# Start phase of a Fourier mixing and Gelu network kernel: second table half later, its negation on GpSimd, the Gelu table loaded late, finer last copies

## The chip, the cores and the metric

The kernel runs on one core of one Trainium2 chip. The metric is the time of one execution on the device in microseconds (us), the median of several runs. TensorE (PE) multiplies matrices and writes into PSUM; VectorE (DVE), ScalarE (ACT) and GpSimd (POOL) work on elements; SyncE (SP) and GpSimd issue the transfers (DMA). Each engine takes its own instructions in order, and engines wait for each other by semaphores.

## The reference

The inputs are `x` (8 images of 3008 x 256), two filter tables of 1505 x 256, and two weight matrices.

```python
X = np.fft.rfft(x, axis=1)                      # x: (8, 3008, 256)
F = (filt_r + 1j * filt_i)[None, :, :]          # (1505, 256)
y = np.fft.irfft(X * F, n=3008, axis=1)
h = y.reshape(24064, 256) @ w_in                # w_in: (256, 2048)
g = 0.5 * h * (1.0 + erf(h / np.sqrt(2)))       # exact Gelu
out = g @ w_out                                 # w_out: (2048, 256), out in float32
```

## The kernel before

The transform of length 3008 = 47 x 64 is done as four table products: along 47 (c1), along 64 (c2, followed by the multiplication with the filters), back along 64 (c3), back along 47 (c4), with transposes between (c1t, c3t). The first image does this on the chip alone, in a start phase; later images do it with transfers through memory, between the matmuls of the network, which runs over 47 tiles of 512 rows (`mm1` with Gelu, `mm2`). The cosine and sine tables are made on the chip as well. Names like `T` or `ps_c` in the profile are these tiles with their numbers left out: `T` is any of T1 to T4.

The buffers in PSUM during the start phase: tag "w" has 2 buffers of two banks each, tag "n" has 4 buffers of one bank. A tag hands out its buffers in turn, and a buffer is free when its last reader is done.

```python
m.psum(wide, w=(2, 2), n=(4, 1))
```

The second table T2 has 24 rows k in two halves of 12. Each half is a sine on ScalarE, a swap (a matmul with a signed permutation, and two copies out of PSUM), and a negation:

```python
def table_2_sin(self, h):
    self.nc.scalar.activation(out=self.T2[:, 12*h:12*h+12, 1, :], in_=self.gen[:, h], func=AF.Sin, scale=2.0*PI)

def table_2_swap(self, h):
    t2 = self.T2[:, 12 * h:12 * h + 12]
    ps = self.bank("ps_sw", "w")
    for i in range(2):
        self.nc.tensor.matmul(ps[:, i, 0:384], lhsT=self.swap, rhs=t2[:, :, 1, 32*i:32*i+32], start=True, stop=True)
    for i in range(2):
        self._evac(t2[:, :, 2, 32*i:32*i+32], ps[:, i, 0:384].rearrange(...), "act", 1.0 - 2.0 * i)

def table_2_minus(self, h):
    t2 = self.T2[:, 12 * h:12 * h + 12]
    self.nc.vector.tensor_scalar(out=t2[:, :, 0, :], in0=t2[:, :, 2, :], scalar1=-1.0, scalar2=None, op0=ALU.mult)

def table_3(self, q, eng):         # 8 transposes of T2 rows into one bank, one copy out
    ps = self.bank("ps_t3", "n", BF16)
    ...
def table_4(self):                 # the weighted tables: 2 small matmuls, 2 small copies on ScalarE
    ps = self.bank("ps_t4", "n")
    ...
def warm_up(self, n):              # matmuls whose result nobody reads
    ps = self.bank("ps_warm", "n")
    for i in range(n):
        self.nc.tensor.matmul(ps, lhsT=self.ones[:, 0:128], rhs=self.ones, start=True, stop=True)
```

`_evac(out, in_, eng, scale)` copies out of PSUM: on ScalarE for "act", on VectorE for False. `dup_filters` copies filter rows from partitions 0-63 to 64-127, two values of k in one copy. The parts of the start phase (all of PSUM tag "n" but c2):

```python
def c1(self, grp, half, eng):      # 4 matmuls from the input x_sb, 1 copy into at_sb
def c1t(self, q, eng):             # 8 transposes of at_sb, 1 copy of 128x1024 into b_sb; needs all of c1
def c2(self, p):                   # 4 matmuls of T2 with b_sb, tag "w"; then the multiplication:
    ...
    if p < 11:
        nc.vector.tensor_tensor(out=w, in0=ps, in1=f..., op=ALU.mult)     # 128x1024
        return
    ...                            # p = 11: two multiplications of 128x512
def c3(self, q):                   # 16 matmuls of T3 with the results of c2(2q) and c2(2q+1)
    ps = [self.bank("ps_c3", "n") for half in range(2)]
    for i, half in ((0, 0), (1, 0), (0, 1), (1, 1), (2, 0), (3, 0), (2, 1), (3, 1)):
        w = self.st[0, "p", 2 * q + i // 2]
        o = 256 * (i % 2) + 128 * half
        for t in range(2):
            self.nc.tensor.matmul(ps[half][:, 128*i:128*i+128], lhsT=w[:, t, o:o+128], rhs=self.T3[:, 4*q+i]..., ...)
    for half in range(2):
        ...                        # one copy of 128x512 into vt_sb for each half
        self._evac(v[:, :, 16*q:16*q+16], ps[half]..., False if q == 5 and half else "act")
```

The order of the start phase:

```python
for k, n in ((0, 4), (4, 8), (12, 12)):
    m.load_filters(k, n)           # transfers issued by GpSimd
m.load_w_in()
...                                # T1p and T1q: two small copies on GpSimd
m.dup_filters(nc.gpsimd, 0, K1)
for u in range(16):
    m.c1(u // 2, u % 2, act if u < 4 or u % 2 and u != 15 else False)
    if u == 3:
        m.warm_up(3)
        m.table_2_sin(0)
    if u == 7:
        m.table_2_swap(0)
        m.table_2_minus(0)
    if u == 11:
        m.table_2_sin(1)
        nc.scalar.activation(out=warm, in_=m.p, func=AF.Gelu)    # brings the Gelu table in
m.load_x(1)                        # the next image, and w_out: transfers issued by GpSimd
m.load_w_out(0)
m.load_w_out(8)
m.c1t(0, False)
m.c1t(1, act)
for q in range(7):
    if q < 6:
        m.c2(2 * q)
        if q == 0:
            m.table_2_swap(1)
        if q + 2 < 6:
            m.c1t(q + 2, act)
        m.c2(2 * q + 1)
    if q == 1:
        m.table_2_minus(1)
    if q < 3:
        m.table_3(q, act)
    if q >= 1:
        m.c3(q - 1)
    if q == 5:
        m.table_4()
...                                # c3t, c4: back along 47; then the network with the other images
```

Of the kernel before, what the change touches and what calls it, by code (L numbers as in the profile page):

```python
# [9 lines left out]
AF = mybir.ActivationFunctionType  # L10
ALU = mybir.AluOpType
# [7 lines left out]
K1 = 24  # L19
HB = 32  # L20
# [8 lines left out]
class _Mix:  # L29
# [159 lines left out]

    def table_2_swap(self, h):  # L190
        t2 = self.T2[:, 12 * h:12 * h + 12]
        ps = self.bank("ps_sw", "w")
        for i in range(2):
            self.nc.tensor.matmul(ps[:, i, 0:384], lhsT=self.swap, rhs=t2[:, :, 1, 32 * i:32 * i + 32],
                                  start=True, stop=True)
        for i in range(2):
            self._evac(t2[:, :, 2, 32 * i:32 * i + 32], ps[:, i, 0:384].rearrange("p (k j) -> p k j", k=12),
                       "act", 1.0 - 2.0 * i)

    def table_2_minus(self, h):  # L200
        t2 = self.T2[:, 12 * h:12 * h + 12]
        self.nc.vector.tensor_scalar(out=t2[:, :, 0, :], in0=t2[:, :, 2, :], scalar1=-1.0, scalar2=None, op0=ALU.mult)

    def weights_4(self, g):

# [30 lines left out]

    def warm_up(self, n):

        ps = self.bank("ps_warm", "n")
        for i in range(n):  # L240
            self.nc.tensor.matmul(ps, lhsT=self.ones[:, 0:128], rhs=self.ones, start=True, stop=True)


    def _evac(self, out, in_, both, scale=None):
# [136 lines left out]
        for c in (slice(0, 128), slice(128, 256)):  # L381
            nc.vector.tensor_tensor(out=w[:, :, :, c], in0=ps[:, :, :, c], in1=f[:, :, :, c], op=ALU.mult)

    def c3(self, q):

        if q == 0:
            self.vt = self.pg.tile([128, 2, 97, 32], BF16, tag="g", name="vt_sb")
        ps = [self.bank("ps_c3", "n") for half in range(2)]
        for i, half in ((0, 0), (1, 0), (0, 1), (1, 1), (2, 0), (3, 0), (2, 1), (3, 1)):
            w = self.st[0, "p", 2 * q + i // 2]  # L390
            o = 256 * (i % 2) + 128 * half
            for t in range(2):
                self.nc.tensor.matmul(ps[half][:, 128 * i:128 * i + 128], lhsT=w[:, t, o:o + 128],  # L393
                                      rhs=self.T3[:, 4 * q + i].rearrange("p a b -> p (a b)"),
                                      start=t == 0, stop=t == 1)
        for half in range(2):
            v = self.vt[:, half, 0:96, :].rearrange("c a b -> c (a b)").rearrange("c (n k) -> c n k", n=HB)
            self._evac(v[:, :, 16 * q:16 * q + 16], ps[half].rearrange("c (k n) -> c n k", n=HB),
                       False if q == 5 and half else "act")

    def c3t(self, u):

# [69 lines left out]
@with_exitstack  # L472
def kernel(
    ctx: ExitStack,
    tc: tile.TileContext,
    x: bass.AP,
    filt_r: bass.AP,
    filt_i: bass.AP,
    moe_w_in: bass.AP,
    moe_w_out: bass.AP,  # L480
    out: bass.AP,
):
    m = _Mix(ctx, tc, x, filt_r, filt_i, moe_w_in, moe_w_out, out)
    nc, B, S = tc.nc, m.B, m.S
    NT = B * S // TCH
    ctx.enter_context(tc.manual_schedule())

    g = m.small
    wide = ctx.enter_context(ExitStack())
    m.psum(wide, w=(2, 2), n=(4, 1))  # L490
    act = "act"
    m.p = m.iota(g, "p", [128, 1], [[0, 1]], cm=1)
    m.load_x(0, 0, 1, (0,))
    m.pi = m.iota(g, "pi", [128, 1], [[0, 1]], cm=1, dt=I32)
    m.load_x(0, 0, 1, (1,))
    m.ones = g.tile([128, 512], BF16, name="ones")
    nc.vector.memset(m.ones, 1.0)
    m.warm_up(10)
    m.table_1(g)
    m.weights_4(g)  # L500
    m.T1c = g.tile([2 * NA, 96], BF16, name="T1c")
    nc.vector.tensor_copy(out=m.T1c.rearrange("p (k h r) -> p k h r", h=2, r=2),
                          in_=m.T1.rearrange("p (h r k) -> p k h r", h=2, r=2))
    m.kk = m.iota(g, "kk", [128, K1 // 2], [[1, K1 // 2]])
    m.jj = g.tile([128, NB], FP32, name="jj")
    for sgn, lo in ((1, 0), (-1, 32)):
        nc.gpsimd.iota(m.jj[:, lo:lo + 32], pattern=[[sgn * NA, 32]], base=min(0, sgn * NA),
                       channel_multiplier=0, allow_small_or_imprecise_dtypes=True)
    cols = m.iota(g, "cols", [128, 128], [[1, 128]])
    m.load_x(0, 1, 4)  # L510
    m.gen = m.py.tile([128, 3, K1 // 2, NB], FP32, tag="y", name="gen")
    m.table_2(g)
    m.table_2_angle(0)
    m.unit_matrices(g, cols)
    m.table_2_angle(1)
    for k, n in ((0, 4), (4, 8), (12, 12)):
        m.load_filters(k, n)
    m.load_w_in()
    m.T1p = g.tile([2 * NA, 2, K1, 2], BF16, name="T1p")
    nc.gpsimd.tensor_copy(out=m.T1p, in_=m.T1.rearrange("p (h r k) -> p h k r", h=2, r=2))  # L520
    m.T1q = g.tile([2 * NA, K1, 2, 2], BF16, name="T1q")
    nc.gpsimd.tensor_copy(out=m.T1q, in_=m.T1.rearrange("p (h r k) -> p k r h", h=2, r=2))
    m.dup_filters(nc.gpsimd, 0, K1)


    warm = g.tile([128, 1], FP32, name="warm")
    for u in range(16):
        m.c1(u // 2, u % 2, act if u < 4 or u % 2 and u != 15 else False)
        if u == 3:
            m.warm_up(3)  # L530
            m.table_2_sin(0)
        if u == 7:
            m.table_2_swap(0)
            m.table_2_minus(0)
        if u == 11:
            m.table_2_sin(1)

            nc.scalar.activation(out=warm, in_=m.p, func=AF.Gelu)
    m.load_x(1)
    m.load_w_out(0)  # L540
    m.load_w_out(8)
    m.c1t(0, False)
    m.c1t(1, act)
    for q in range(7):
        if q < 6:
            m.c2(2 * q)
            if q == 0:
                m.table_2_swap(1)
            if q + 2 < 6:
                m.c1t(q + 2, act)  # L550
            m.c2(2 * q + 1)
        if q == 1:
            m.table_2_minus(1)
        if q < 3:
            m.table_3(q, act)
        if q >= 1:
            m.c3(q - 1)
        if q == 5:
            m.table_4()
    wide.close()  # L560
    wide = ctx.enter_context(ExitStack())
    m.psum(wide, v=(5, 1), t=(3, 1))
    for u in range(10):
        if u < 8:
            m.c3t(u)
        if u >= 2:
            m.c4(u - 2, (act, False if u > 7 else act))
    wide.close()
    m.psum(ctx, h=(3, 1), o=(2, 1), f=(3, 1))


    at = {}

    def put(slot, f, *a):
        at.setdefault(slot, []).append((f, a))

    def first(b):
        return (b * S // TCH) * 16

    for b in range(1, B):  # L580
        hi = first(b)
        if b == 1:
            s1, n1, r1, s2, n2, r2, s4, n4 = 0, 1, 16, 26, 2.8, 61, 68, 0.72
        else:
            s1, n1, r1, s2, n2, r2, s4, n4 = hi - 94, 1, hi - 78, hi - 69, 3.7, hi - 23, hi - 17, 1
        for u in range(16):
            put(s1 + int(u * n1), m.s1, b, u)
            put(s4 + int(u * n4), m.s4, b, u // 2, u % 2)
        for c in range(4):
            put(r1, m.r1, b, c)  # L590
            put(r2, m.r2, b, c)
        for p in range(12):
            put(s2 + int(n2 * p), m.s2, b, p)
            put(s2 + int(n2 * p) + 4, m.s3, b, p)
        if b + 1 < B:
            for i in range(8):
                put(s2 + int(n2 * (i + 2)), m.load_next, b, i + 2, i // 2, i % 2)

    for s in range((NT + 1) * 16):
        t, jc = s // 16, s % 16  # L600
        for f, a in at.pop(s, ()):
            f(*a)
        if t >= 1:
            m.mm2(t - 1, jc)
        if t < NT:
            m.mm1(t, jc)
    assert not at
# [30 lines left out]
```

## Time and profile before

| what | value |
|---|---|
| time, median of 3 runs | 784.98 us (784.55 to 786.02) |
| span of the profiled execution | 784.6 us |
| first matmul with w_in (end of the start phase) | 43.70 us after the start |
| Gelu table load | 1.28 us, at 14.19 |
| one multiplication c2 (128x1024, VectorE) | 1.21 us |
| one filter copy on GpSimd (64x1024), 12 of them | 1.035 us, 17.6 to 29.5 |
| negation on VectorE | 0.35 us at 11.8, 1.24 us at 24.5 |

A line of the page's groups names the source line, the engine, the operation, output and input; the chain of waits follows back from the last instruction what released each step; the timeline gives start, length and, in brackets, how long the engine was idle before and what ended that. The stretches of time give each engine's busy us in a stretch and the clock that TensorE was granted, 1.00 being full.

### The profile page before, as it was taken

Reading aid. Unit: us, or ns where it says so; the run is one execution under the profiler, and the core shown is the slowest. Engines: PE = TensorE matmul, PEld = TensorE weight load, DVE = VectorE, ACT = ScalarE, POOL = GpSimd, SP = SyncE. Lnnn points to the kernel's source line nnn. Section 1 sums busy time; section 2 is a strip of 40 time slices with the busy share of each in tenths; the row PEclk is TensorE's granted clock in tenths of the full one; section 3 lists DMA queues with packets and bytes.
Section 4 is the critical chain, followed back from the end, with each engine's and each line's share of the span. In section 5 each row is a group of like instructions: output and inputs, shape, how many; then the busy total and the mean of one; then the engine's idle time right before and its main releaser. Section 6 shows DMA issues by size and latency. Waiting matters only on the chain.

```text
span 784.6 us, 14712 instructions
## 1 busy us (share of the span) xinstructions
PE 769.8 (98%) x5931; PEld 538.9 (69%) x5931; DVE 404.5 (52%) x720; ACT 567.5 (72%) x975; POOL 64.2 (8%) x156
## 2 busy tenths in 40 slices
PE   6899999999999999999999999999999999999997
PEld 4867676676776767667677776667767676766666
DVE  6875756364554645556454664536645366411011
ACT  5789955897558875588755986568965788566663
POOL 7801100010000100001000110001100000000000
PEclk8999999999999999999999999999999999999999
DMA  9775843565344661446615465254642521510111
GB/s 150 142 137 141 153 122 101 144 113 138 84 107 131 133 143 51 118 141 120 158 36 159 108 115 148 61 169 87 127 125 74 152 81 55 135 41 28 41 41 54
DMA packets 86213, 85.63 MB, mean 109 GB/s; under 512 B 5761, under 2 KB 76417, under 8 KB 86145
## 3 DMA queue, kind: packets, MB, share of 16 engines
q1 hardware_dynamic: 77760, 68.70, 31.2%
q0 software_dynamic: 8384, 16.00, 14.3%
q8 instruction: 46, 0.75, 0.4%
q14 instruction: 23, 0.18, 0.1%
HBM read 54.00 MB, written 46.66 MB: 128 GB/s over the span
## 4 chain that ended last, share of the span: by engine, by line
PE 94%; DMA 3%; DVE 1%; ACT 1%; POOL 0%; issue 0%; SPq 0%; DVEq 0%; POOLq 0%
PE ps_o L463 41%; PE ps_h L449 40%; PE ps_s L262 3%; PE ps_s L335 3%; PE ps_s L310 2%; PE ps_s L285 2%; DMA d_sb<-R 2%; PE ps_c L373 1%; DMA x_sb<-in_x_dram 1%; PE ps_c L393 1%; PE ps_c3t L412 0%; DMA R<-v_sb 0%; POOL x_sb L82 0%; PE ps_c L426 0%; PE ps_c1t L361 0%
## 5 line engine op out<-in xcount | busy, mean ns | idle before, releaser
L452 ACT ACTIVATE g_sb<-ps_h 128x512 bf16<-128x512 f32 x752 | 439.4, 597 | 189.9 <-PE ps_h L449 179.0
L463 PE MATMUL ps_o<-w_out_sb,g_sb 128*128 128x256 bf16 x3008 | 449.0, 272 | 0.0
L449 PE MATMUL ps_h<-y_sb,w_in_sb 128*128 128x512 bf16 (+3 forms) x1600 | 447.6, 366 | 0.5 <-DVE y_sb L251 0.5
L463 PEld LDWEIGHTS <-g_sb 128*128 128x128 bf16 x3008 | 287.6, 98 | 133.7
L449 PEld LDWEIGHTS <-w_in_sb 128*128 128x128 bf16 x1600 | 155.0, 98 | 23.3 <-issue 0.8
L467 DVE COPY ost<-ps_o 128x512 f32<-128x512 f32 x94 | 64.4, 685 | 125.2 <-PE ps_o L463 124.7
L293 DVE TENSOR_TENSOR p<-ps_s,F 128x512 bf16<-128x512 f32 x84 | 58.1, 692 | 103.7 <-ACT p L292 97.2
L251 DVE TENSOR_SCALAR y_sb<-ps_s 128x376 bf16<-128x376 f32 x112 | 61.0, 548 | 82.5 <-PE ps_s L335 82.5
L249 DVE CAST a_sb<-ps_s 96x512 bf16<-96x512 f32 x112 | 76.3, 685 | 40.9 <-PE ps_s L262 40.9
L249 DVE CAST v_sb<-ps_s 128x512 bf16<-128x512 f32 x84 | 57.6, 687 | 12.9 <-PE ps_s L310 12.4
L291 ACT ACTIVATE p<-ps_s 64x512 bf16<-64x512 f32 x84 | 49.9, 594 | 2.1
L335 PEld LDWEIGHTS <-d_sb 96*128 96x128 bf16 x448 | 30.3, 97 | 28.8 <-issue 3.1
L292 ACT CAST p<-ps_s 64x512 bf16<-64x512 f32 x84 | 48.5, 577 | 1.0
L101 POOL COPY gate<-p 1x1 bf16<-1x1 bf16 x48 | 8.5, 176 | 482.4 <-DVE p L295 482.4
L262 PE MATMUL ps_s<-x_sb,T 94*96 94x512 bf16 x112 | 42.7, 381 | 0.0
L335 PE MATMUL ps_s<-T,d_sb 96*128 96x94 bf16 x448 | 36.3, 204 | 1.9 <-DMA d_sb<-R 1.7
L295 DVE TENSOR_TENSOR p<-p 128x512 bf16<-128x512 bf16 x84 | 35.7, 425 | 2.9
L294 DVE TENSOR_TENSOR p<-p,F 128x512 bf16<-128x512 bf16 x84 | 34.9, 416 | 0.0
L82 POOL DMA_DIRECT2D x_sb<-in_x_dram x64 | 32.5, 510 | 13.0 <-issue 10.9
L310 PE MATMUL ps_s<-p,T 128*128 128x256 bf16 x168 | 32.1, 273 | 0.0
L285 PE MATMUL ps_s<-b_sb,T 128*128 128x256 bf16 x168 | 32.1, 273 | 0.0
L310 PEld LDWEIGHTS <-T 128*128 128x128 bf16 x168 | 16.4, 98 | 20.0 <-DVE p L295 0.5
(96 smaller groups left out, 191.0 us busy)
## 6 DMA issues: line engine op xcount, KB each, us to landing
out_dram<-ost SPq DMA_DIRECT2D x94, 256.0 KB, 2.5
x_sb<-in_x_dram POOLq DMA_DIRECT2D x64, 188.0 KB, 3.9
R<-a_sb SPq DMA_DIRECT2D x56, 192.0 KB, 3.0
b_sb<-R SPq DMA_DIRECT2D x28, 384.0 KB, 4.6
R<-v_sb SPq DMA_DIRECT2D x42, 256.0 KB, 4.0
d_sb<-R SPq DMA_DIRECT2D x56, 192.0 KB, 4.6
w_in_sb<-in_moe_w_in_dram POOLq DMA_DIRECT2D x2, 512.0 KB, 9.2
w_out_sb<-in_moe_w_out_dram POOLq DMA_DIRECT2D x2, 512.0 KB, 11.2
```

What stands on the lines that cost most here:

```text
L249: self.nc.vector.tensor_copy(out=out, in_=in_)
L251: self.nc.vector.tensor_scalar(out=out, in0=in_, scalar1=scale, scalar2=None, op0=ALU.mult)
L262: nc.tensor.matmul(ps[0:96, :], lhsT=self.T1, rhs=self.st[b, "x"][:, 2 * u:2 * u + 2, :], start=True, stop=True)
L291: nc.scalar.activation(out=p2[0:64], in_=ps[64:128], func=AF.Copy, scale=-1.0)
L292: nc.scalar.copy(out=p2[64:128], in_=ps[0:64])
L293: nc.vector.tensor_tensor(out=p1, in0=ps, in1=f(0), op=ALU.mult)
L310: nc.tensor.matmul(ps[:, 256 * i:256 * i + 256], lhsT=self.T3[:, k].rearrange("p a b -> p (a b)"), rhs=w[:, 256 * i:256 * i + 256], start= ...
L335: nc.tensor.matmul(ps[:, 94 * i:94 * i + 94], lhsT=d[:, (grp % 2) * 4 + i, 128 * half:128 * half + 128], rhs=t4, start=True, stop=True)
L449: nc.tensor.matmul(ps[:, o:o + n], lhsT=self.w_in_sb[:, dc, jc * 128:jc * 128 + 128], rhs=self.ring[:, dc, off:off + n], start=(dc == 0), ...
L452: nc.scalar.activation(out=self.st["g", t][:, jc, :], in_=ps, func=AF.Gelu)
L463: nc.tensor.matmul(ps[:, tile_i % 2, :], lhsT=g[:, jc, tile_i * 128:tile_i * 128 + 128], rhs=self.w_out_sb[:, jc, :], start=(jc == 0), sto ...
L467: nc.vector.tensor_copy(out=ost, in_=ps)
```

## The change

The sine of the second half of T2 moves behind the last input part, and its swap and negation behind the first two products; that negation goes to GpSimd. The Gelu table load moves from the input stage to the product stage, behind c3 of products 6 and 7; the weighted tables (`table_4`) move two rounds forward to q = 3. The first two filter copies go to VectorE, the others stay on GpSimd, in two groups. The swap takes two "n" buffers instead of one "w", the warm-up matmuls take "w" and become more. The last c3 round is cut into two of one product each, with copies half as wide. The purpose is to let the products start earlier and to shorten what follows the last product. What is computed is the same.

```diff
     def table_2_swap(self, h):
-        ps = self.bank("ps_sw", "w")
         for i in range(2):
-            self.nc.tensor.matmul(ps[:, i, 0:384], lhsT=self.swap, rhs=t2[:, :, 1, 32 * i:32 * i + 32],
+            ps = self.bank("ps_sw", "n")
+            self.nc.tensor.matmul(ps[:, 0:384], lhsT=self.swap, rhs=t2[:, :, 1, 32 * i:32 * i + 32],
...
-    def table_2_minus(self, h):
+    def table_2_minus(self, eng, h):
-        self.nc.vector.tensor_scalar(...)
+        eng.tensor_scalar(...)
...
     def warm_up(self, n):
-        ps = self.bank("ps_warm", "n")
+        ps = self.bank("ps_warm", "w")
...
-    def c3(self, q):
+    def c3(self, p, np=2):              # np products from p on, product by product
...
-                       False if q == 5 and half else "act")
+                       False if p == 11 and half else "act")
...
+    m.dup_filters(nc.gpsimd, 4, 8)
     m.T1p = ...
-    m.dup_filters(nc.gpsimd, 0, K1)
     for u in range(16):
-        m.c1(u // 2, u % 2, act if u < 4 or u % 2 and u != 15 else False)
+        m.c1(u // 2, u % 2, act if u < 4 or u % 2 else False)
         if u == 7:
             m.table_2_swap(0)
-            m.table_2_minus(0)
+            m.table_2_minus(nc.vector, 0)
+            m.warm_up(3)
         if u == 11:
-            m.table_2_sin(1)
-            nc.scalar.activation(out=warm, in_=m.p, func=AF.Gelu)
-    m.load_x(1)
-    m.load_w_out(0)
-    m.load_w_out(8)
+            m.warm_up(2)
+    m.table_2_sin(1)
+    m.warm_up(2)
     m.c1t(0, False)
     m.c1t(1, act)
+    m.dup_filters(nc.vector, 0, 4)
     for q in range(7):
         if q < 6:
             m.c2(2 * q)
-            if q == 0:
-                m.table_2_swap(1)
-            if q + 2 < 6:
+            if q > 0 and q + 2 < 6:
                 m.c1t(q + 2, act)
             m.c2(2 * q + 1)
-        if q == 1:
-            m.table_2_minus(1)
-        if q < 3:
+        if q == 0:
+            m.table_3(0, act)
+            m.table_2_swap(1)
+            m.table_2_minus(nc.gpsimd, 1)
+            m.dup_filters(nc.gpsimd, 12, 12)
+            m.load_x(1)
+            m.load_w_out(0)
+            m.load_w_out(8)
+            m.c1t(2, act)
+        if 1 <= q < 3:
             m.table_3(q, act)
         if q >= 1:
-            m.c3(q - 1)
-        if q == 5:
+            if q < 6:
+                m.c3(2 * q - 2)
+            else:
+                m.c3(10, 1)
+                m.c3(11, 1)
+        if q == 3:
             m.table_4()
+        if q == 4:
+            nc.scalar.activation(out=warm, in_=m.p, func=AF.Gelu)
```

## The prediction

> **What bounds the kernel now.** I read the page first: engine totals, then the slices.
>
> ```profile
> PE 769.8 (98%) x5931; PEld 538.9 (69%) x5931; DVE 404.5 (52%) x720; ACT 567.5 (72%) x975; POOL 64.2 (8%) x156
> ```
>
> TensorE is busy for all but about 15 us of 784.6. The changed lines belong to a start phase that is over when the first product with w_in begins at 43.70 us (chain of waits). From there on both programs are the same, about 741 us of TensorE work. So the change can only move the start of that body: this is a question of a few us at most, 0.1 to 0.5%, and never of 2% (15.7 us).
>
> Next the chain of waits for 10 to 45 us, each line giving start, length and work:
>
> ```profile
> 13.44 0.73 ACT T L187
> ...
> 14.19 1.28 ACT L538
> ...
> 15.48 0.20 ACT warm L538
> 15.68 0.39 ACT at_sb L247
> ...
> 16.12 1.78 PE ps_c1t L361 x15
> 17.90 0.94 PE ps_c L373 x4
> 18.84 0.61 PE ps_sw L194 x2
> ...
> 19.47 0.88 ACT T L247 x2
> ...
> 20.39 0.61 PE ps_c L373 x4
> ...
> 21.10 1.24 DVE p L378
> ```
>
> ScalarE has the sine of the second table half (L187), the Gelu table load with its dummy activation (L538), and only then the copy of an input part (at_sb) that the transposes c1t need. Products start (L373), then the swap (L194) and its two copies hold the next product (20.39). Its PSUM tag "w" has two buffers and the swap took one, so the second product could not have its buffer before. The second multiply on VectorE starts at 21.10, against 18.93 for the first.
>
> Then the clock, from the stretches of time (columns: stretch, its length, busy us of PE, PEld, DVE, ACT, POOL, then granted clock, DMA share, GB/s):
>
> ```profile
> 14.00:17.00 3.00, 1.78 (x18) 1.38 (x16) 1.08 (x3) 2.03 (x4) 3.00 (x7) 0.50 1.02 163
> 17.00:20.00 3.00, 2.88 (x23) 2.08 (x21) 1.76 (x2) 1.56 (x3) 2.94 (x6) 0.62 1.12 171
> ```
>
> The matmuls of the chain's slowest part run at half clock: four product matmuls take 1.01 us at 17.82, but 0.60 later. Last, the timeline of the product stage:
>
> ```profile
> 21.27 0.60 PE L373 MATMUL ps_c<-b_sb,T 128*128 128x256 bf16 x4
> ...
> 24.50 1.24 DVE L202 TENSOR_SCALAR T<-T 128x768 bf16<-128x768 bf16 x1
> ...
> 31.64 0.60 PE L373 MATMUL ps_c<-b_sb,T 128*128 128x256 bf16 x4
> ...
> 36.14 1.50 PE L412 MATMUL ps_c3t<-eye,vt_sb 128*128 128x128 bf16 x24 [0.78 <-DVE vt_sb L249]
> ```
>
> These are product c2(2), the negation, product c2(10), and the first transposes of the next stage. I compare these marks below.
>
> [...]
>
> **The change part by part.** Marks are us from the start of the span.
>
> (1) The input stage ends earlier. The last input parts are there at about 12.98, when their first matmuls run; the last matmul ends at 14.61 (a group of eight starts at 13.77 and takes 0.84). Two more warm-ups follow the swap and unit 11. At full clock four matmuls with their weights take about 0.25 us, not 0.42, so I put the last matmul at 14.2 to 14.4 and the last copy (0.49 on ScalarE, no table load or sine ahead of it) at 14.9. Before, that copy ended at 16.07: 1.2 us.
>
> (2) c1t(0) from 15.0 takes 0.61, the VectorE copy 0.69 (its row at 17.08), so 16.35. Now c2(0) on TensorE (0.60) and two filter copies on VectorE run beside each other. A VectorE filter copy has no row; from the 0.35 us of the 768-element negation I estimate 0.4 for 1,024, so two end at 17.15. The filters themselves are there: GpSimd's third-group loads, which wait on the first group, leave one behind the other from 13.70 to 15.35. First multiply at 17.2 instead of 18.93.
>
> (3) The swap takes "n" banks, so c2(1) follows c2(0) at once, 17.1 to 17.7, and the second multiply starts at 18.35 instead of 21.10. A multiply is issued each 1.14 us (seven in 8.00).
>
> (4) Then TensorE has eight table transposes (0.45), the swap (0.35), and c1t(2) (0.45; its bank is free when ScalarE has copied c1t(1), 17.15): c2(2) at 19.0 instead of 21.27, 2.3 us earlier.
>
> (5) From c2(2) to c2(10) the kernel before takes 31.64 - 21.27 = 10.37 us. TensorE's own order sets that: the steps between pairs of products are 2.88, 2.77, 2.46 and 2.26. The negation (1.24) leaves VectorE, but the chain shows TensorE there, so I count nothing for it: VectorE needs 2 x 1.14 = 2.28 a pair and will wait about 0.5 us a pair in its place. The two weighted-table matmuls come in (0.25). c2(10) at 29.6, 2.0 earlier.
>
> (6) ScalarE, which now carries the Gelu load in this stage. From the copy of table 3 at 18.35, by issue intervals (1,024-wide copies 0.91, pairs of vt copies 0.96): 3 x 0.91 + 0.80 (swap) + 4 x 0.91 + 5 x 0.96 + 0.45 (weighted tables) + 1.40 (Gelu) + 0.60 + 0.30 (the finer last copies) = 14.7. That ends at 33.1, and with about 0.9 us of waits for the eighth product group at 34.0. So ScalarE nearly becomes the bound, but does not pass the rest.
>
> (7) The end. Multiplies 10 and 11 end at 31.7 and 32.9. With single products in the last two groups, only 0.25 us of matmuls and one narrow copy (0.35 to 0.4) remain: 33.7 to 34.0. The next stage starts at about 34.05 instead of 36.14.
>
> (8) GpSimd. Four filter copies of 1.035 from 17.3 (landing of the second filter group), two table copies 0.66, then the negation, estimated at 768/1024 x 1.035 = 0.8, then the six others. The negation ends at 22.9, the filters of product 6 at 23.9, wanted at about 25. The loads of the next image start at 29.2 against 29.53 before. Nothing here ends last.
>
> Sum: 36.14 - 34.05 = 2.1 us of start phase. 785.0 - 2.1 = 782.9; I round to 783.0, because hand schedules miss waits more often than they invent them.
>
> **Rivals.** *ScalarE is the bound and eats the gain.* For it: it is busy 4.74 and 4.83 of 5 us in 20 to 30 already, and 1.4 us of Gelu move into its stage. If its copies took their full 1.03 and 0.55 without overlap, (6) would be 16.8 and the end 35.3: gain 0.8, 784.2. Against: successive copies start 0.92 apart (21.47 and 22.39), and it waits 2.5 us for TensorE between 30 and 35, where the load is now placed.
>
> [...]
>
> *The clock does not stay up.* If the added warm-ups are too few, c1 to c2(0) run at half clock as before, about 0.3 + 0.3 + 0.4: gain about 1.1, 783.9.
>
> *GpSimd's negation is slow.* Over 2 us it would hold product 6. Its copies of 1,024 take 1.035, which speaks against.
>
> *The body gives something back.* The next image's loads start no earlier, while the body wants them 2 us sooner (first use 42.80 before, about 40.7 after). Eight loads leave from 29.2 in 4.0 us and land in 5.7 (median), the last near 39. It should hold; a miss is under 1 us.
>
> **Range and chances.** The mechanism may give 0.8 to 2.8 us, and the three times before spread over 1.5 us (784.55 to 786.02), which makes a median uncertain by some 0.4. So 781.9 to 784.5 for 8 in 10. Faster by over 2% would need 769.3 or less and slower 800.7 or more; neither lies in reach of a 43 us phase: 0.01 each, 0.98 within.
>
> **What would show it right or wrong.** Right: no table load before the transposes c1t; clock near 1.0 between 12 and 19; first two multiplies at about 17.2 and 18.4 with no gap; product c2(2) near 19.0 and c2(10) near 29.6; the transposes L413 near 34.0; span from there unchanged at 748.5. Wrong: a VectorE filter copy of over 1 us; ScalarE without a gap from 18 to 35; multiply 6 waiting on GpSimd; the first w_in product less than 1 us earlier than 43.70; or TensorE waiting for x_sb behind it.

## The result and the profile after

| | kernel before | changed kernel | ratio, 95% interval |
|---|---|---|---|
| first comparison, median us | 785.5 | 784.71 (783.76 to 785.21) | 0.9989 [0.9972, 1.0006] |
| second comparison (38 and 13 executions) | 785.63 | 785.32 | 0.9997 [0.9988, 1.0006] |
| third comparison (60 and 19 executions) | 785.26 | 784.27 | 0.9989 [0.9982, 0.9996] |
| span of the execution in the profile | 784.6 | 781.9 | |
| first product with w_in begins, us | 43.70 | 40.98 | |

By the ratios, the time is lower by 0.2 to 0.9 us; the second comparison alone can't tell it from zero. The start phase gave about what it was to give: its end comes 2.7 us earlier in these two profiles, and 2.1 us in the mean of all profiles of the two kernels. Less than half of this reached the end.

The chain of waits of the changed kernel, 10 to 45 us (start, length, work):

```profile
14.27 7.07 DMA F<-in_filt_i_dram
...
21.42 0.23 POOL T1p L522
21.66 0.29 POOL T1q L524
21.95 2.13 POOL T L201
...
24.13 1.04 POOL F L96
25.19 1.24 DVE p L377
...
28.91 1.08 ACT vt_sb L246 x2
30.01 1.28 ACT L571
...
33.43 1.50 PE ps_c3t L413 x24
...
40.98 0.59 PE ps_h L450 x2
```

The chain of before went from ScalarE's table load through the first products on TensorE. That stretch is gone. The chain now goes through GpSimd: two copies of table parts, the negation (L201), and one filter copy (L96), for which a multiply on VectorE (L377) waits. Ahead of these the chain names a filter load, but GpSimd's timeline shows that its own copies fill that time: from 17.36 on it pauses for no more than 0.1 us at a time, and that first copy had waited for the second group of filters.

```profile
17.36 3.97 POOL L96 COPY F<-F 64x1024 bf16<-64x1024 bf16 x4 [0.72 <-DMA F<-in_filt_i_dram]
```

After GpSimd come ScalarE's copies with the Gelu load (L571), and the transposes L413 begin at 33.43, against 36.14 before.

The stretches of time, with the columns of the prediction's table (the two after the busy times are the granted clock and the DMA share):

```profile
14.00:17.00 3.00, 2.61 (x34) 2.31 (x34) 2.14 (x5) 1.93 (x3) 2.64 (x5) 1.00 1.05 157
17.00:20.00 3.00, 3.00 (x43) 2.60 (x40) 3.00 (x4) 2.90 (x5) 2.64 (x3) 1.00 1.15 151
```

The clock is 1.00 in both, against 0.50 and 0.62 before. TensorE's timeline gives the two marks of the product stage, c2(2) and c2(10), which were at 21.27 and 31.64:

```profile
17.67 0.60 PE L372 MATMUL ps_c<-b_sb,T 128*128 128x256 bf16 x4
...
28.93 0.60 PE L372 MATMUL ps_c<-b_sb,T 128*128 128x256 bf16 x4
```

VectorE's timeline in the same stage (in brackets the idle time before, and what ended it):

```profile
15.56 0.77 DVE L96 COPY F<-F 64x1024 bf16<-64x1024 bf16 x2
16.36 4.62 DVE L377 TENSOR_TENSOR p<-ps_c,F 128x1024 bf16<-128x1024 f32 x4
...
21.23 2.36 DVE L377 TENSOR_TENSOR p<-ps_c,F 128x1024 bf16<-128x1024 f32 x2 [0.26 <-issue]
25.19 5.75 DVE L377 TENSOR_TENSOR p<-ps_c,F 128x1024 bf16<-128x1024 f32 x5 [1.60 <-POOL F L96]
```

Multiplies start at 16.36 and four follow each other without a gap. But multiply 6 waits 1.60 us for a filter copy of GpSimd, and GpSimd was late because of one instruction:

```profile
21.92 2.14 POOL L201 TENSOR_SCALAR T<-T 128x768 bf16<-128x768 bf16 x1
```

In all three profiles of the changed kernel, multiply 6 starts 7.8 us after GpSimd's first filter copy (17.36, 17.86, 18.09), and the first product with w_in 15.8 us after multiply 6. So here the moment at which the filters land decides the end of the start phase, and it differs by 0.7 us between executions.

Behind the start phase, the view of waits has TensorE's waits for the loads of d_sb, a tile that the kernel writes to the DRAM tensor R as v_sb and reads back in another layout (us in total, times, longest). In the kernel before:

```profile
PE ps_s L335 <- DMA d_sb<-R: 1.7, 4, 0.5
```

In the changed kernel:

```profile
PE ps_s L334 <- DMA d_sb<-R: 2.2, 3, 1.8
```

One wait, of 1.8 us, is new: before, none was longer than 0.5. It belongs to image 2. On TensorE's timeline, before:

```profile
195.74 0.33 PE L335 MATMUL ps_s<-T,d_sb 96*128 96x94 bf16 x4 [0.52 <-DMA d_sb<-R]
```

and after:

```profile
194.17 0.33 PE L334 MATMUL ps_s<-T,d_sb 96*128 96x94 bf16 x4 [1.76 <-DMA d_sb<-R]
```

No line of the diff touches image 2.

**A sum that holds for every kernel here.** In all 18 profiles of this study (two of before, three of the changed kernel, thirteen of variants of either), span = begin of the first product with w_in + TensorE's waits for data read back from R (d_sb, and in two variants once b_sb) + a rest between 738.5 and 739.2 us. Before: 784.6 - 43.70 - 1.7 = 739.2. After: 781.9 - 40.98 - 2.2 = 738.7. So only the first two terms are open to question, and the experiments are read by them. A profile shows a single execution, though, and executions of one kernel differ by two us and more (783.89 to 787.15 in the 38 of the kernel before), so differences under 1 us are taken from the medians.

### The profile page after: what moved, and what is told of

It is laid out like the page before. It is cut to its first block, busy times and chain, and to the rows that moved or that the text cites. A ratio compares the mean times of both kernels' runs of the same rounds, so it can differ in the third digit from the quotient of the medians.

```text
span 781.9 us, 14728 instructions
## 1 busy us (share of the span) xinstructions
PE 769.3 (98%) x5938; PEld 538.1 (69%) x5938; DVE 403.1 (52%) x720; ACT 567.5 (73%) x978; POOL 64.7 (8%) x155
## 4 chain that ended last, share of the span: by engine, by line
PE 93%; DMA 3%; POOL 1%; DVE 1%; ACT 0%; issue 0%; SPq 0%; POOLq 0%; DVEq 0%
PE ps_o L464 41%; PE ps_h L450 41%; PE ps_s L261 3%; PE ps_s L334 3%; PE ps_s L309 2%; PE ps_s L284 2%; DMA d_sb<-R 1%; DMA F<-in_filt_i_dram 1%; DMA x_sb<-in_x_dram 1%; PE ps_c3t L413 0%; DMA R<-v_sb 0%; POOL x_sb L82 0%; PE ps_c L427 0%; POOL T L201 0%; ACT vt_sb L246 0%
## 5 line engine op out<-in xcount | busy, mean ns | idle before, releaser
L309 PEld LDWEIGHTS <-T 128*128 128x128 bf16 x168 | 16.3, 98 | 20.1 <-DVE p L294 0.5
## 6 DMA issues: line engine op xcount, KB each, us to landing
x_sb<-in_x_dram POOLq DMA_DIRECT2D x64, 188.0 KB, 3.9
```

Source lines behind the costliest of these rows:

```text
L309: nc.tensor.matmul(ps[:, 256 * i:256 * i + 256], lhsT=self.T3[:, k].rearrange("p a b -> p (a b)"), rhs=w[:, 256 * i:256 * i + 256], start= ...
```

## The experiments

**Theory.** The reordering shortens the start phase by about 2 us. Part of that is given back in the body, because the change adds instructions to TensorE (7 warm-up matmuls with their 7 weight loads; 11,862 become 11,876). Instructions come in by transfers of the same 16 DMA engines that carry the data: the page of each of the two kernels has `q8 instruction: 46, 0.75, 0.4%` among its queues (packets, MB, share of the 16 engines' span). More instructions ahead shift the moments of all later fetches, and one of these now falls in front of a write that TensorE will wait for. **Rivals.** The start phase gains less than it seems, as GpSimd's negation or the Gelu load takes it back. Or the difference is only one of the reference and of repeated measurement.

The kernels are told in an order that serves reading, not the order in which they ran. Where nothing else is said, an edit is to the changed kernel. "Mark" is the begin of the first product with w_in.

### Both kernels again

No edit. The kernel before:

> The kernel before against itself, to learn what is the same program's spread, and a second profile of it. Theory A: ratio 1.000 within 0.0007; the first w_in product between 43 and 44 us again, body 740.9. Theory B: the start phase of this program varies by over 1 us between profiles (first w_in product outside 43 to 44.5), so the first pair of profiles was no fair measure.

785.73 against 785.63, ratio 1.000 [0.9992, 1.0008]; mark 43.25, waits for d_sb 2.4 in five pieces, the longest 0.9.

The changed kernel, unaltered:

> The changed kernel once more, unaltered, timed in five rounds beside the kernel before. Theory A (the start phase is shorter by the 2.7 us that the two profiles show at the first w_in product, 40.98 against 43.70, and the median of four runs was blurred by a spread of 1.5 us among runs): 2.0 to 2.7 us faster than the kernel before, ratio 0.9965 to 0.9975, and the first w_in product again at 40.5 to 41.5. Theory B (about 2 us are given back in the body, or come and go in the start phase from run to run): 0.5 to 1.2 us faster, ratio 0.9985 to 0.9994, and the profile shows either a later first w_in product or a body longer than 740.9 us.

785.32 against 785.63, 0.9997 [0.9988, 1.0006]; mark 41.49, waits 3.1 in six pieces. Beside the kernel before once more:

> The changed kernel, unaltered, on one chip beside three others already timed apart. Theory F (start phase about 2 us shorter, some 0.8 us of it lost to the fetch in front of image 2's last write): 0.3 to 1.3 us under the kernel before, ratio 0.9984 to 0.9997; wait for d_sb of image 2 at 1.2 to 1.8 us.

784.27 against 785.26, 0.9989 [0.9982, 0.9996]; mark 41.72, waits 1.9. The mark is at 43.48 in the mean of the two profiles of before and at 41.40 in the three of after. So the start phase is 2.1 us shorter, and 0.2 to 0.9 us of that are seen at the end. The small result is not a chance of the first comparison.

### The 14 instructions alone

The kernel before, with 14 more instructions on TensorE at the very start (7 narrow warm-up matmuls, each with its weight load), and nothing else of the change. `warm_up` gets a width:

```diff
-    m.warm_up(10)
+    m.warm_up(9)
+    m.warm_up(8, 64)
```

> The kernel before with as many TensorE instructions as the changed one: the last of its ten opening warm-ups is replaced by eight of 64 columns, 14 instructions more in the same time; all else as before. Theory F: the fetch now falls on the same write of image 2 as in the changed kernel, the write lands in 3.3 to 3.6 us instead of 2.3 to 2.4, the wait for d_sb there goes from 0.5 to 0.9 up to 1.2 to 1.8 us, and the time is 0.7 to 1.0 us over the kernel before, ratio 1.0008 to 1.0013. Rival R: nothing moves, wait 0.5 to 0.9 us, ratio 1.000.

786.21 against 785.06; the ratio, which is not simply the quotient of these two medians, is 1.0010 [1.0002, 1.0018]. Beside the changed kernel:

> The kernel before with 14 more TensorE instructions, once more. Theory F: wait for d_sb of image 2 at 1.2 to 1.8 us, ratio 1.0005 to 1.0015, and so 1.5 to 2.3 us over the changed kernel, which has the same fetch position and differs by the start phase alone.

785.97 against 785.26, 1.0011 [1.0003, 1.0020]. Both times the kernel before is slower by 0.8 to 0.9 us with them, and the start phase isn't: the mark is at 42.81 and 42.88, somewhat earlier than in before. The wait of image 2 has come, as in the changed kernel:

```profile
195.91 0.33 PE L336 MATMUL ps_s<-T,d_sb 96*128 96x94 bf16 x4 [1.66 <-DMA d_sb<-R]
```

The DMA view shows where it comes from. The last write of v_sb of image 2, in the kernel before, from 189 us on (queue with kind: packets, MB, share; then an issue with its size and the us to its landing):

```profile
q1 hardware_dynamic: 766, 0.50, 62.6%
...
R<-v_sb SPq DMA_DIRECT2D x1, 256.0 KB, 2.3
```

With the 14 instructions, from 187 us on:

```profile
q8 instruction: 1, 0.02, 1.0%
...
R<-v_sb SPq DMA_DIRECT2D x1, 256.0 KB, 3.9
```

And in the changed kernel, from 186.2 to 190.1 us:

```profile
GB/s 0 0 0 0 0 0 168 0 0 74 252 289 273 236 278 299 305 263 305 300 320 331 320 347 336 347 174 58 21 21 21 21 21 32 21 21 32 21 21 21
...
q8 instruction: 1, 0.02, 2.4%
...
R<-v_sb SPq DMA_DIRECT2D x1, 256.0 KB, 3.6
```

A transfer of the instruction queue (the single spike of 168 GB/s, in the seventh of forty slices) comes right before the write. Most of the write is done in about 2 us. Then a stream of 21 GB/s remains for about 1 us, and there is no such tail in the kernel before. In the second profile with the 14 instructions the tail is at 20 to 25. Probably it is the share of the one DMA engine that had the fetch first. Two estimates from these lines speak for it: the fetch, a single packet, took 2.4% of 16 engines' 3.9 us, about 1.5 us of one of them, and a sixteenth of 347 GB/s, the highest slice, is 21.7. The trace doesn't name the engine of a packet. The write lands after 3.6 instead of 2.3 us, the loads of d_sb wait for it, and TensorE for them. Before, the nearest fetch comes at 191.8, when the write of 189.0 has landed.

The pages of the two kernels have 46 such transfers with 0.75 MB, so 16 KB each. For the 11,862 instructions on TensorE that is about 258 a transfer, an estimate from these numbers. The wait of image 2 goes with the moment of one of them: 0.52 us in the kernel before, with the fetch at 191.8, 1.76 in the changed kernel, with the fetch at 186.9, 0.7 behind the issue of the write.

### The start phase without the 14 instructions

```diff
             m.table_2_minus(nc.vector, 0)
-            m.warm_up(3)
-        if u == 11:
-            m.warm_up(2)
     m.table_2_sin(1)
-    m.warm_up(2)
```

> The changed kernel without the seven warm-up matmuls that the change adds (three behind the swap, two behind unit 11, two behind the input stage). It then has as many TensorE instructions as the kernel before. Two things are told apart. Clock: if the added warm-ups are what keeps the clock up, it falls to half between about 12 and 19 us as in the kernel before (mean clock 0.993 to 0.996), and the first w_in product comes at 42.0 to 42.6, about 1 us later than in the changed kernel; if not, the clock stays at 0.999 and the mark at 40.8 to 41.5. Fetch: the write of image 2 lands in about 2.4 us and TensorE waits 0.9 us or less for d_sb there. Time: with a lost clock and a saved wait about that of the changed kernel, 785; with a kept clock 784.0 to 784.5.

783.72 against 785.34, 0.9976 [0.9967, 0.9985]. The view of waits:

```profile
PE ps_s L334 <- DMA d_sb<-R: 0.3, 1, 0.3
```

The warm-ups had another purpose, the clock, and the stretches show that it is lost without them, 0.57 where the changed kernel has 1.00:

```profile
14.00:16.00 2.00, 1.39 (x15) 1.35 (x14) 0.87 (x3) 1.35 (x3) 2.00 (x4) 0.57 1.15 168
16.00:18.00 2.00, 2.00 (x16) 1.49 (x14) 1.74 (x4) 1.02 (x1) 1.96 (x4) 0.57 1.09 158
```

```profile
25.51 5.90 DVE L377 TENSOR_TENSOR p<-ps_c,F 128x1024 bf16<-128x1024 f32 x5 [0.46 <-PE ps_c L372]
```

The first multiply comes at 17.52, which is 1.16 us later than in the changed kernel, but multiply 6 at 25.51 (25.19 in the changed kernel) and the mark at 41.30 (mean of after 41.40), where 42.0 to 42.6 was expected for a lost clock. Multiply 6 now waits for TensorE's product and no more for GpSimd's copy, which ends at 25.28. So a clock of 0.57 from 14 to 18 us cost about 0.2 us at the mark, an estimate from these two times: where the clock is full, GpSimd's chain holds multiply 6 anyway.

With this, start phase and instructions stand in a square, as ratios to the kernel before:

| | 11,862 instructions | 14 more |
|---|---|---|
| start phase of before | 1 | 1.0010 and 1.0011 |
| new start phase | 0.9976 | 0.9989, 0.9997 and 0.9989 |

Down a column, the start phase is worth 0.0024 without the instructions and 0.0013 to 0.0022 with them, that is 1.9 and 1.0 to 1.7 us. Along a row, the instructions cost 0.0010 to 0.0011 and 0.0013 to 0.0021, that is 0.8 to 0.9 and 1.0 to 1.6 us. Each ratio is uncertain by about 0.0009, and the kernels of the square were not all timed on one chip, though each beside the kernel before on its own. That both rows and both columns agree in direction, and roughly in size, is what speaks.

### Other numbers of instructions

30 more than in the changed kernel (`warm_up(10)` becomes `warm_up(5)` and `warm_up(20, 128)`):

> The changed kernel with five of its ten opening warm-ups cut into twenty of 128 columns, 30 instructions more in the same time. By the positions of the fetches in the traces so far, this puts the one of image 2 about 1.6 us ahead of the last write and that of image 3 behind its loads. Theory F: waits for d_sb of images 2 and 3 of at most 0.9 us each, and a time 0.6 to 1.0 us under the changed kernel's: 1.0 to 1.8 us under the kernel before, ratio 0.9977 to 0.9987. If the shift only moves the collision to another image again, as the 60 instructions did, the time stays within 0.4 of the changed kernel's.

783.77 against 785.34, 0.9978 [0.9970, 0.9987]; mark 41.44, waits for d_sb 1.2, none of them for image 2. Beside the changed kernel:

> The changed kernel with 30 more TensorE instructions, once more, now beside the changed kernel on the same chip. Theory F: 0.5 to 1.2 us under the changed kernel, wait for d_sb of image 2 of 0.9 us or less. If the time of one and the same program differs by 1 us from one loading to the next, the gap between the two may vanish while the waits stay as they were; then the time alone does not carry the theory.

783.95 against 785.26, 0.9979 [0.9972, 0.9986], when the changed kernel had 0.9989 [0.9982, 0.9996]; mark 41.55, waits 0.7. The intervals still touch. Beside the changed kernel of the same comparison the fetch comes 1.4 us earlier (186.6 against 188.0). It was expected 1.6 us ahead of the write's issue and starts only 0.3 to 0.4 ahead, but it is over before the write's packets begin to move, 0.9 us behind the issue, and the write lands after 2.3 us.

60 more (`warm_up(40, 128)`):

> The changed kernel with its ten opening warm-up matmuls of 512 columns cut into forty of 128: the same time on TensorE before the first input part, but 60 more instructions (30 weight loads, 30 matmuls). Theory F (a fetch of 256 TensorE instructions, one 16 KB transfer, falls on one transfer engine just when the last half spectrum of image 2 is written, lands it 1.3 us later, and so TensorE waits 1.25 to 1.76 us for d_sb at 194 us instead of 0.5 to 0.9): with 60 more instructions that fetch comes about 5 us earlier, the write lands in about 2.4 us instead of 3.6, the wait for d_sb of image 2 is 0.9 or less and the time is 0.5 to 1.1 us lower than the changed kernel's. Rival R (the wait is longer because the start phase is shorter, as transfers are now late against the matmuls): the wait stays at 1.2 to 1.8 us whatever the number of instructions, and the time is the changed kernel's within 0.4 us.

784.85 against 785.06, 0.9996 [0.9988, 1.0004]; mark 41.44. The expected gain of 0.5 us or more over the changed kernel is missing. Image 2 doesn't wait any more (its fetch came at 184.0), but image 3 waits 1.27 us, its fetch at 283.3 behind a write issued at 282.4, and one load of b_sb 0.93 at 525 us. So more instructions are neither good nor bad. What counts here is whether a fetch meets a write. Issue of the last write of image 2, start of the nearest fetch, landing and wait:

| kernel | write issued | fetch | landing | wait |
|---|---|---|---|---|
| before | 189.0 | 191.8 | 2.3 | 0.52 |
| before, again | 188.7 | 191.7 | 2.3 | 0.87 |
| before with 14 more | 188.1 | 189.5 | 3.9 | 1.66 |
| after | 186.2 | 186.9 | 3.6 | 1.76 |
| after, again | 186.9 | 187.5 | 3.1 | 1.25 |
| after, side by side | 187.4 | 188.0 | 3.1 | 0.96 |
| after with 30 more, side by side | 187.0 | 186.6 | 2.3 | 0.24 |
| after with 60 more | 187.3 | 184.0 | 2.3 | none |

The packets of this write begin to move 0.9 us behind its issue. Each of the 18 profiles holds seven such writes, the last one of v_sb of each image but the first: 126 in all. Behind 12 of them a fetch starts 0.6 to 1.4 us after the issue, and these land after 3.1 to 3.9 us; TensorE then waits 0.8 to 1.8 us for d_sb. For 7 of them the fetch starts between 0.2 us ahead of the issue and 0.3 behind it, and they land after 2.4 to 2.9. The other 107 land after 2.3 to 2.4, and no other wait for d_sb is longer than 0.9.

### GpSimd's negation

The negation on VectorE, behind the second pair of products:

```diff
             m.table_2_swap(1)
-            m.table_2_minus(nc.gpsimd, 1)
...
+        if q == 1:
+            m.table_2_minus(nc.vector, 1)
```

> The negation of the second half goes back to VectorE, behind the multiplication of product 3; all else as changed. Theory G (GpSimd's 2.13 us negation holds product 6): GpSimd's filter copy for product 6 ends at about 23.1, multiply 6 starts at about 24.6 (VectorE then carries 0.35 to 1.24 us more), the first w_in product comes 0.3 to 0.8 us earlier. Rival (VectorE is as tight as GpSimd and the negation meets a filter copy there): no change within 0.2 us, with a negation of 1.2 us or more on VectorE.

783.8, 0.9986 [0.9975, 0.9998]. VectorE's timeline:

```profile
21.26 0.57 DVE L201 TENSOR_SCALAR T<-T 128x768 bf16<-128x768 bf16 x1
...
24.39 2.36 DVE L377 TENSOR_TENSOR p<-ps_c,F 128x1024 bf16<-128x1024 f32 x2 [0.31 <-PE ps_c L372]
```

It takes 0.57 us there instead of 2.14, multiply 6 starts at 24.39 and waits for TensorE, no more for GpSimd, and the mark comes at 40.19, 1.2 us ahead of the changed kernel's mean. The 14 instructions are still there, and image 2 waits 1.59 us. In the same comparison the changed kernel had 0.9997 [0.9988, 1.0006], which makes the negation worth 0.0011, or 0.9 us. But the intervals overlap, and against the changed kernel's other ratio, 0.9989, hardly anything is left.

GpSimd again, but with a plain copy of the same tile (it leaves out the minus sign of that half of the table):

```diff
+        if eng is self.nc.gpsimd:
+            eng.tensor_copy(out=t2[:, :, 0, :], in_=t2[:, :, 2, :])
```

> The changed kernel with a plain copy on GpSimd in place of the negation of the second half: same tiles, same rows of 64 in a stride, same 768 elements, but no arithmetic (the output leaves out the sign in half of the second table). If the operation is what costs 2.14 us, the copy takes 0.7 to 0.9 us and multiply 6 starts about 1.3 us earlier; if the strided rows cost it, the copy also takes 1.8 us or more.

```profile
22.10 0.82 POOL L202 COPY T<-T 128x768 bf16<-128x768 bf16 x1
```

One execution, 783.04 us, multiply 6 at 24.24 and the mark at 40.03. So it isn't the tile, its layout or GpSimd's place in time that makes 2.14 us, but the operation.

The table copies ahead of four filter copies on GpSimd:

```diff
-    m.dup_filters(nc.gpsimd, 4, 8)
     m.T1p = ...
     nc.gpsimd.tensor_copy(out=m.T1q, ...)
+    m.dup_filters(nc.gpsimd, 4, 8)
```

> The two small table copies on GpSimd (0.55 us together) go ahead of its first four filter copies, where it waits 0.72 us for filters anyway. If the chain through GpSimd's negation (2.13 us) and the filter copy behind it sets the time of multiply 6, multiply 6 starts at about 24.6 instead of 25.19 and the first w_in product comes 0.4 to 0.6 us earlier than in the changed kernel; the time is 0.4 to 0.6 us lower. If ScalarE's order with the Gelu load sets the end instead, multiply 6 is earlier but the first w_in product moves by less than 0.2.

784.11 against 785.63, 0.9977 [0.9968, 0.9986]; mark 41.03. The sought effect is missing: the filters landed later in that execution, the copies began at 17.89 (17.36 in after), the negation at 21.97 (21.92), multiply 6 at 25.24 (25.19). Nothing in the trace explains the lower time. So beside the changed kernel again:

> The changed kernel with the two table copies first, once more. Its number of TensorE instructions is the changed kernel's and its trace showed the same marks, so by theory F its time is the changed kernel's within 0.5 us. If it is again 1 us or more faster, there is a cause that the traces so far do not show.

783.66, 0.9982 [0.9976, 0.9989], when the changed kernel had 0.9989 [0.9982, 0.9996]; mark 41.24, waits 2.2. The lead shrinks from 1.2 us to 0.6, and the intervals, apart in the second comparison ([0.9968, 0.9986] and [0.9988, 1.0006]), overlap here. Whether this order is worth anything stays open. It counts against the theory as the whole account: these two profiles have the changed kernel's 14 instructions and the late write of image 2 (landing after 3.3 and 3.9 us, waits of 1.44 and 1.60), and yet the ratios are near those of the kernels without it (0.9976 to 0.9979).

### The Gelu load out of the product stage

```diff
-        if q == 4:
-            nc.scalar.activation(out=warm, in_=m.p, func=AF.Gelu)
+    nc.scalar.activation(out=warm, in_=m.p, func=AF.Gelu)      # behind the q loop
```

> The changed kernel with its Gelu table load (1.28 us and the dummy activation 0.20) moved once more, behind the last vt copy, where ScalarE waits 2.0 us for the first product of c4. If the load sits on the path to the first transposes L413, as the chain of the changed kernel has it (30.01 to 31.51, between vt copies), the last vt copy ends 0.8 to 1.4 us earlier, and the first w_in product comes 0.5 to 0.8 us earlier (limited by multiply 11, which ends at 32.14, then a narrow product and copy of 0.8, against 33.4 now): 0.5 us lower than the changed kernel. If VectorE's chain through multiply 6 sets the end, less than 0.2.

784.05 against 785.06, 0.9986 [0.9978, 0.9995]. The load starts at 34.12, behind the last copies. The mark, expected 0.5 to 0.8 us earlier, comes at 41.78, as the filters landed late in this execution (GpSimd's first copy at 18.38, multiply 6 at 26.22). From multiply 6 to the mark it takes 15.56 us, against 40.98 - 25.19 = 15.79 in the changed kernel. So the load in the chain at 30.01 costs 0.2 us, not its 1.28: at that place ScalarE now waits 1.18 us for a product.

### Both with other numbers of instructions

Negation on VectorE, Gelu behind the loop, and 60 instructions more:

> The changed kernel with the negation back on VectorE, the Gelu load behind the last vt copy, and the 60 more TensorE instructions. If the three effects are what their own runs suppose, they add: first w_in product at 39.3 to 39.9 us instead of 41 to 41.5, wait for d_sb of image 2 at most 0.9, time 782.0 to 783.0, ratio to the kernel before 0.995 to 0.997. If the parts hide one another: 783.3 to 784, no better than the negation alone.

783.13 against 785.06, 0.9975 [0.9965, 0.9985]; mark 39.98. In the same comparison the 60 instructions alone had 0.9996 [0.9988, 1.0004], so the two edits are worth 0.0021, or 1.6 us, and the marks differ by 1.46. The chain view names the loads of the next image at this mark (a load that landed at 39.98). But TensorE begins the transposes L414 at 32.42 here, and from there to the mark it takes 7.56 us, as in the kernel before (7.56) and in the changed kernel (7.55). So the products' chain ends the start phase here too, and the load held nothing up. The ratio and the mark miss what was expected by a little (0.997 at most, 39.9 at most); image 3 waits 0.82, with a fetch behind its last write. With 30 instructions more:

> The changed kernel with the negation on VectorE, the Gelu load behind the last vt copy, and 30 instead of 60 more TensorE instructions. Start phase as in the combined kernel before it (first w_in product at 39.3 to 40.0), waits for d_sb of at most 0.9 us each: ratio 0.995 to 0.997, at or under that one's 0.9975. If the number of instructions has no say, the same 0.9975 within 0.0008.

782.34 (782.16 to 783.61) against 785.34, 0.9964 [0.9952, 0.9977]: the lowest ratio of all, 2.8 us below the kernel before, from five executions; the interval overlaps that of the kernel with 60 more. Mark 40.57, later than the expected 39.3 to 40.0, as the filters landed late (GpSimd's first copy at 18.40); waits for d_sb 1.0 and for b_sb 0.3.

## Why the prediction was wrong

It said 783.0, between 781.9 and 784.5. Measured were 784.71.

**The step that failed** is the frame around the sum: "From there on both programs are the same, about 741 us of TensorE work", and with it "span from there unchanged". The instructions behind the mark are the same, but the 741 us are not fixed. They are 738.5 to 739.2 us, and the waits for data read back from R, which were between 0.3 and 3.1 us in the profiles. The change shifts the instruction fetches against the writes by 14 TensorE instructions, and that gave back 0.8 to 1.6 us (the rows of the square). Point (1) counted the warm-up matmuls only as a gain. In the two profiles of the first pair the step even seems right, with 784.6 - 36.14 = 748.5 and 781.9 - 33.43 = 748.5: there the new 1.2 us in front of image 2 happen to be made up by smaller waits elsewhere and by the rest. It is the medians, of which each stands for many executions, that show it wrong: they fell by 0.3 to 1.0 where the start phase fell by about 2.

Of the error of 1.7 us, about 0.5 is the reference (785.0 was a median of three, 785.5 stood beside the result). The other 1.2 is gain that is missing: 2.0 predicted, 0.8 measured. The cost of the instructions, 0.8 us in the kernel before, is the largest known part of it; the ratios don't carry a finer split.

That the start phase as a whole came out near the predicted 2.1 us is partly luck: the first multiply came 0.8 us earlier than predicted, and the negation, 1.3 us longer than estimated, took more than that back. With the negation on VectorE the mark is at 40.19, 1.2 us ahead of the changed kernel's mean.

**The steps by themselves:**

- (1) The clock was 1.00 between 14 and 20 us, as predicted. That the added warm-ups would hold it there was my assumption, which no view of the kernel before shows; without them it was 0.57 from 14 to 18 us. But the full clock was hardly needed: without them the mark is later by about 0.2 us only. (In the kernel before the clock was 0.50 from 12.4 to 19.3.)
- (2) First multiply 16.36, predicted 17.2. The two filter copies on VectorE took 0.77 us together, predicted 0.8.
- (3) The second multiply followed without a gap, as predicted.
- (4), (5) c2(2) 17.67 and c2(10) 28.93, predicted 19.0 and 29.6. The lead of 1.3 us at c2(2) was half gone at c2(10), where multiply 6 had waited.
- (6) ScalarE neared the bound without setting it: 0.2 us for the Gelu load, as shown. The rival that had it eat 1.3 us fell. (Its 16.8 us is also a slip: with the durations that it names the sum is about 16.3.)
- (7) Transposes L413 at 33.43, predicted about 34.05; mark 40.98 (mean 41.40). From the one to the other it took 7.55 us, as before (43.70 - 36.14 = 7.56).
- (8) The negation was mis-sized: 0.8 estimated, 2.14 measured, since I scaled a copy and not a multiplication. It starts at 21.92, 0.2 before the predicted moment, and "Nothing here ends last" was false. The rival "Over 2 us it would hold product 6" came true. The negation on VectorE and the later Gelu load together bring 1.6 us (against the 60 instructions alone).
- "The body gives something back" was among the rivals, but with the wrong cause: it named x loads, and the waits are for d_sb.

**What stays open.** The profiled executions of before lie 1.0 and 0.7 us above their medians, those of before with 14 more instructions 1.0 and 0.8 below, so the waits of single profiles can't be added to the medians. Summed over all images, the waits for d_sb in the kernel with 14 more instructions are 2.0 and 1.9 us, no more than in before (1.7 and 2.4), as its other waits were smaller in those executions. That the 14 instructions cost 0.8 us is measured. That a write with a fetch 0.6 to 1.4 us behind its issue lands late (3.1 to 3.9 us, 12 of 12) and that TensorE then waits 0.8 to 1.8 us is shown. That this is the whole 0.8 is only probable: the kernel with the table copies first has the same fetch and the same wait, and is 0.6 to 1.2 us under the changed kernel. Nor is it known why repeated measurements of one kernel differ by up to 0.0008.

## What to carry to other kernels

When a change is worth less than some us, instructions added far ahead of a critical transfer count as a part of the change (14 of them cost 0.8 us here): test them alone, by adding as many to the kernel before, and by leaving them out of the new one. A step moved to another engine needs a duration of that same operation on that engine; a copy of equal size isn't one (0.82 us for the copy on GpSimd here, 2.14 for the multiplication). Before feeding the clock with warm-up matmuls, look whether the stretch at half clock is what ends last (here it cost about 0.2 us). And where the chain of waits names a transfer, compare with what else the instruction needed: here it once named a load that held nothing up.

## What the runs showed of the hardware

- GpSimd took 2.14 us for a bf16 multiplication by -1 of 128x768, 0.82 for the copy of the same tile. VectorE took 0.57 for the same multiplication in the variant that only moves it there, and 0.35, 0.87 and 1.24 in three other profiles.
- A 256 KB write with an instruction fetch of 16 KB that started 0.6 to 1.4 us behind its issue landed after 3.1 to 3.9 us, against 2.3 to 2.4 for writes without a fetch from 0.2 us ahead of the issue to 1.4 behind it (12 and 107 writes). In the changed kernel a stream of 21 GB/s came last.
- A clock of 0.57 on TensorE, in the mean from 14 to 18 us, cost about 0.2 us at the end of the phase, as GpSimd's chain was nearly as long.
